# A fused attention and MLP kernel, rewritten with an order of engines from a model, wider exps, value bursts, paired key sums and token-major W2

## The chip, the cores and the metric

The kernel runs on one core of one Trainium2 chip. The metric is the device time of one execution in microseconds (us). Every time below is the median of several executions, with the lowest and highest of them. TensorE (PE) multiplies matrices, VectorE (DVE) and ScalarE (ACT) work on elements, GpSimd (POOL) does small work, and SyncE (SP) issues DMA transfers. Both kernels write the results of matmuls to PSUM, an on-chip tensor that they divide into eight banks.

## The reference, cut to what matters

```python
def _layernorm(x, eps=1e-5):
    m = mean(x); v = var(x)
    return (x - m) / sqrt(v + eps)

x  = A_x                                   # 2048 tokens x 1024, bf16
xn = _layernorm(x)
# A: attention, 32 heads of 32
q, k, v = split(xn @ wqkv)
s = softmax(q @ k.T * 32 ** -0.5) @ v @ wo
# B: MLP with a layer norm of its own, F = 3584
y = _layernorm(xn)                         # so x is normalised twice
g = silu(gelu(y @ w1 + b1) @ w2 + b2)
return x + s * g
```

The second norm of an already normalised token is only a scale s per token. With v the first variance and r = 1/sqrt(v + eps), the scale is 1/sqrt(v r r + eps). Both kernels use that, in different ways.

Attention is cut into 512 units. A unit is one group of four heads, 256 queries and 256 keys. It has 8 score matmuls, exps over 128 x 2048 values, and then value matmuls and matmuls with a matrix of ones, which sum the exps for the softmax's denominator. A query group is eight units with the same heads and queries.

## The kernel before

The order of instructions is written by hand: scores and exps of unit b, values of unit b-2, then dense matmuls (projections or MLP) up to a budget of time.

```python
for bl in range(NBH):                                # one unit
    ...                                              # 8 score matmuls into 4 of 5 PSUM banks
    for j in range(4):                               # four exps of 128 x 512
        add("scalar", lambda en, ...: en.activation(Pb[b % NPB][:, j, :], bank(bk), ACT.Exp, scale=SCALE), ...)
    if b >= 2:
        emit_pv(b - 2)                               # values and ones of one unit, in one accumulator bank
    ...                                              # dense matmuls for per_batch_ns
```

```python
# emit_pv, at the end of a query group: the reciprocal of 256 columns, then the product
add("vector", lambda en: en.reciprocal(rc_t[ri][:], ps[:, ACCB * 512 + 256:ACCB * 512 + 256 + QW]), ...)
add("vector", lambda en: en.tensor_tensor(OT[:, hg, ...], ps[:, ACCB * 512:ACCB * 512 + QW], rc_t[ri][:], op=ALU.mult), ...)
```

```python
# prologue: the normalised x and the doubly normalised x, each transposed on TensorE (256 transposes)
add("vector", lambda e, ...: e.tensor_scalar(xnb[i2][:], xt, lnp[:, tb, 2:3], lnp[:, tb, 3:4], op0=ALU.mult, op1=ALU.add), ...)
add("gpsimd", lambda e, ...: e.tensor_scalar(ybb[i2][:], xt, lnp[:, tb, 6:7], lnp[:, tb, 7:8], op0=ALU.mult, op1=ALU.add), ...)
```

The softmax here doesn't subtract the row's maximum and nothing guards it: scores larger than these inputs give would overflow.

Of the kernel before, what the change touches and what calls it, by code (L numbers as in the profile page):

```python
# [12 lines left out]
ENGS = ("sync", "gpsimd", "tensor", "vector", "scalar")  # L13


class _Sched:

    def __init__(self, nc, stack):
        self.nc = nc
        self.stack = stack  # L20
        self.ops = {e: [] for e in ENGS}
        self.sems = {}
        self.counts = {}

    def sem(self, name):
        if name not in self.sems:
            self.sems[name] = self.stack.enter_context(self.nc.semaphore(name))
            self.counts[name] = 0
        return name

    def cnt(self, name):
        return self.counts.get(name, 0)

    def add(self, eng, fn, waits=(), inc=None, dma=False):
        val = None
        ws = []
        if inc is not None:
            self.sem(inc)
            if dma and self.counts[inc] > 0:
                ws.append((inc, self.counts[inc]))  # L40
            self.counts[inc] += 16 if dma else 1
            val = self.counts[inc]
        for w in waits:
            if w is None:
                continue
            s, v = w
            if v is None or v <= 0:
                continue
            self.sem(s)
            ws.append((s, v))  # L50
        self.ops[eng].append((fn, tuple(ws), inc, dma))
        return val

    def emit(self, eng_name, eng):
        waited = {}
        for fn, waits, inc, dma in self.ops[eng_name]:
            for (s, v) in waits:
                if waited.get(s, 0) >= v:
                    continue
                eng.wait_ge(self.sems[s], v)  # L60
                waited[s] = v
            if fn is None:
                continue
            ins = fn(eng)
            if inc is not None:
                ins.then_inc(self.sems[inc], 16 if dma else 1)


def bass_recurrent_scan__mha_block__mixer_channel_mlp__prompt_kernel(
# [10 lines left out]
):  # L80
    _, S, D = A_x.shape
    F = B_w1.shape[1]
    DH = 32
    H = D // DH
    HG = H // 4
# [3 lines left out]
    QW = 256  # L89
    NQB = S // QW  # L90
    NKBP = S // 256
    CW = 256
    NCH = S // CW
    NH5 = D // 512
    EPS = 1e-5
    SCALE = DH ** -0.5
    W1P = 256
    NPC = F // W1P
    FBP = W1P // 128
    NPB = 4  # L100
    assert HG == DC and S % 512 == 0 and F % W1P == 0 and D % 512 == 0 and NT % 4 == 0

    x2 = A_x.rearrange("b s d -> (b s) d")
    out2 = out.rearrange("b s d -> (b s) d")

    with ExitStack() as st:
        sc = _Sched(nc, st)
        add = sc.add

        def sb(name, shape, dt):  # L110
            return st.enter_context(nc.sbuf_tensor(name, list(shape), dt))

        yT_d = nc.dram_tensor("yT_scratch", (128, DC, S), BF16).ap()
        g_d = nc.dram_tensor("g_scratch", (S, D), BF16).ap()

        ident = sb("ident", [128, 128], BF16)
        iota_i = sb("iota_i", [128, 128], I32)
        ones = sb("ones", [128, 32], BF16)
        xnT = sb("xnT", [128, DC, S], BF16)
        OT = sb("OT", [128, HG, S], BF16)  # L120
        QT = [sb(f"QT{i}", [128, S], BF16) for i in range(2)]
        KT = [sb(f"KT{i}", [128, S], BF16) for i in range(2)]
        Vh = [sb(f"Vh{i}", [128, NT, 128], BF16) for i in range(2)]
        wsl = [sb(f"wsl{i}", [128, DC, 3, 128], BF16) for i in range(2)]
        Pb = [sb(f"Pb{i}", [128, 4, 512], BF16) for i in range(NPB)]
        ar_state = {"off": 0}
        ARENA_ELEMS = (2 * DC * CW + 2 * DC * W1P + FB * CW + 2 * FB * 128 + DC * CW + 2 * D
                       + 3 * (6 * FBP * CW) + 3 * (4 * CW))
        arena = sb("arena", [128, ARENA_ELEMS], BF16)

        def carve(shape, dt, reset=False):
            if reset:
                ar_state["off"] = 0
            n = 1
            for d_ in shape[1:]:
                n *= d_
            nbf = n * (2 if dt == F32 else 1)
            off = ar_state["off"]
            ar_state["off"] += nbf
            assert ar_state["off"] <= ARENA_ELEMS, (ar_state["off"], ARENA_ELEMS)  # L140
            v = arena[:, off:off + nbf]
            if dt == F32:
                v = v.bitcast(F32)
            if len(shape) == 3:
                v = v.rearrange("p (a b) -> p a b", a=shape[1])
            return v

        yTc = [carve([128, DC, CW], BF16) for i in range(2)]
        w1p = [carve([128, DC, W1P], BF16) for i in range(2)]
        off_hT = ar_state["off"]  # L150
        hT = carve([128, FB, CW], BF16)
        off_after_hT = ar_state["off"]
        if FB * CW >= 4 * D + 2 * DC * 128:
            ar_state["off"] = off_hT
            xnb = [carve([128, D], BF16) for i in range(2)]
            ybb = [carve([128, D], BF16) for i in range(2)]
            yTs = [carve([128, DC, 128], BF16) for i in range(2)]
            assert ar_state["off"] <= off_after_hT
            ar_state["off"] = off_after_hT
        else:  # L160
            xnb = [sb(f"xnb{i}", [128, D], BF16) for i in range(2)]
            ybb = [sb(f"ybb{i}", [128, D], BF16) for i in range(2)]
            yTs = [sb(f"yTs{i}", [128, DC, 128], BF16) for i in range(2)]
        w2s = [carve([128, FB, 128], BF16) for i in range(2)]
        gT = carve([128, DC, CW], BF16)
        gst = [carve([128, D], BF16) for i in range(2)]
        xb_t = [carve([128, FBP * CW], F32) for i in range(3)]
        u_t = [carve([128, FBP * CW], F32) for i in range(3)]
        th_t = [carve([128, FBP * CW], F32) for i in range(3)]
        zh_t = [carve([128, CW], F32) for i in range(3)]  # L170
        th2_t = [carve([128, CW], F32) for i in range(3)]
        ofin = [carve([128, 512], F32, reset=(i == 0)) for i in range(2)]
        obf = [carve([128, D], BF16) for i in range(2)]
        NTB = 4
        xnT_flat = xnT[:].rearrange("p c s -> p (c s)")
        wo_sb = xnT_flat[:, 0:HG * D].rearrange("p (c n) -> p c n", c=HG)
        xres = [xnT_flat[:, HG * D + i * D: HG * D + (i + 1) * D] for i in range(NTB)]
        gres = [xnT_flat[:, HG * D + (NTB + i) * D: HG * D + (NTB + i + 1) * D] for i in range(NTB)]
        assert HG * D + 2 * NTB * D <= DC * S
        rc_t = [sb(f"rc{i}", [128, QW], F32) for i in range(2)]  # L180
        b1T = sb("b1T", [128, FB], F32)
        b2h = sb("b2h", [128, DC], F32)
        stats = sb("stats", [128, NT, NH5, 6], F32)
        mv = sb("mv", [128, NT, 2], F32)
        lnp = sb("lnp", [128, NT, 8], F32)
        ps = st.enter_context(nc.psum_tensor("ps", [128, 8 * 512], F32))
# [3 lines left out]

        def bankb(i):
            return ps[:, i * 512:(i + 1) * 512].bitcast(BF16)

        ACCB = 5
        NRING = 5

        add("gpsimd", lambda e: e.iota(iota_i[:], pattern=[[1, 128]], base=0, channel_multiplier=-1), inc="c_iota")
        add("vector", lambda e: e.tensor_single_scalar(ident[:], iota_i[:], 0, op=ALU.is_equal),
            waits=[("c_iota", 1)], inc="c_ident")
        add("vector", lambda e: e.memset(ones[:], 1.0), inc="c_ones")  # L200
        add("gpsimd", lambda e: e.dma_start(b1T[:], B_b1.rearrange("(fb p) -> p fb", p=128)), inc="c_b1", dma=True)
        add("gpsimd", lambda e: e.dma_start(b2h[:], B_b2.rearrange("(nb p) -> p nb", p=128)), inc="c_b2", dma=True)
        add("vector", lambda e: e.tensor_scalar_mul(b2h[:], b2h[:], 0.5), waits=[("c_b2", 16)], inc="c_b2h")

        def evy(tb):
            return ("ev_xyd", tb + 1)

        xst_v = OT[:].rearrange("p g s -> p (g s)")
        for tb in range(NT):
            add("sync" if tb % 2 == 0 else "gpsimd",  # L210
                lambda e, tb=tb: e.dma_start(xst_v[:, tb * D:(tb + 1) * D], x2[tb * 128:(tb + 1) * 128, :]),
                inc=f"x_ld{tb % 4}", dma=True)
        HALF = NT // 2 if NT >= 8 else NT

        def emit_stats(tb):
            xt = xst_v[:, tb * D:(tb + 1) * D]
            for c in range(NH5):
                add("vector", lambda e, tb=tb, c=c, xt=xt: e.bn_stats(stats[:, tb, c, :], xt[:, c * 512:(c + 1) * 512]),
# [578 lines left out]
```

## Time and profile before

The kernel before took 1485.49 us (1482.51 to 1490.63, three runs).

| | before |
|---|---|
| span of the profiled run | 1486.1 us |
| PE / ACT / DVE busy | 1205.9 / 1143.5 / 702.2 us |
| until the first exp | 107 us |
| 512 units | 107 to 1400 us, 2.53 us each |
| after the last unit | 86 us, ACT idle |

These lines are from the page of the kernel before: the busy time of the engines with its share of the span; the chain of work that ended last, by engine; and three of the costliest groups. A group reads: line, engine, operation, tiles and shapes, count, then busy us, mean ns of one, and the idle time just before it with what ended most of it.

```profile
PE 1205.9 (81%) x30330; PEld 801.9 (54%) x30336; DVE 702.2 (47%) x1173; ACT 1143.5 (77%) x2246; POOL 102.7 (7%) x119
...
PE 40%; ACT 18%; DVE 17%; DMA 14%; issue 10%; POOL 1%; DVEq 0%; SPq 0%; ACTq 0%; POOLq 0%
...
L695 ACT ACTIVATE Pb<-ps 128x512 bf16<-128x512 f32 x2048 | 1058.7, 609 | 173.2 <-PE ps L686 166.1
...
L302 PE MATMUL ps<-arena 128*32 128x256 bf16 x14336 | 494.0, 282 | 87.9 <-DMA arena<-in_B_w_dram 66.8
...
L612 DVE RECIPROCAL rc<-ps 128x256 f32<-128x256 f32 x64 | 112.4, 1756 | 145.8 <-PE ps L605 145.8
```

No engine is full, and the chain passes from one to another. ScalarE's 2048 exps wait for scores, TensorE's dense matmuls wait 66.8 us for weights, and each query group ends with a reciprocal of 1.76 us.

The view of the waits gives engine, line, what it waited for, us in total, times, and the longest.

```profile
PEld ps L686 <- ACT Pb L695: 186.4, 402, 2.9
...
PE ps L302 <- DMA arena<-in_B_w_dram: 66.8, 58, 5.3
```

**An accounting of TensorE's span.** It is worked out from the trace. Matmuls stream at 109 ns for a quad of four with 256 columns and 216 ns for a quad with 512 (start to start in the timeline; the few transposes are counted in proportion). A burst of scores uses another tiling of the array than everything else. In the trace of before, the time from the last column quad to the scores is about 320 ns in the median where the next quad would take 109, and from the scores to the values 0.11 us more than streaming, so I count 0.325 us a burst for the two switches. What remains of the span is called rest: TensorE waits, or runs at half clock. For the kernel before: streaming 970, switches 166, rest 350 us (71 until 107 us, 269 in the middle, 10 after 1422 us).

### The profile page before, as it was taken

To read this page: it belongs to the slowest core of one execution; us is meant where nothing else is said; L and a number is where in the kernel's file an instruction comes from. 1 tells how busy PE (TensorE), PEld (TensorE's weight loads), DVE (VectorE), ACT (ScalarE), POOL (GpSimd) and SP (SyncE) were. 2 spreads that over 40 slices of the span, in tenths; PEclk is the share of its full clock that TensorE was granted. 3 is DMA by queue.
4 is the path that set the end of the run, shared out by engine and by line. 5 is a ranking of instruction groups with operands and counts; after the bars stand their busy time and mean duration, and the time that the engine had idled before them with its cause. 6 is when DMAs were issued, how large, how long until landed. Compare 5 with 4: busy or idle time off the path is not lost.

```text
span 1486.1 us, 65842 instructions
## 1 busy us (share of the span) xinstructions
PE 1205.9 (81%) x30330; PEld 801.9 (54%) x30336; DVE 702.2 (47%) x1173; ACT 1143.5 (77%) x2246; POOL 102.7 (7%) x119
## 2 busy tenths in 40 slices
PE   2589878887889878987798878988798878777887
PEld 1455656555556545565555555655455655555643
DVE  6532862257422772347522683238522682277233
ACT  1229988897889888988898989988898987687600
POOL 3320000000000100001000100001000000000057
PEclk9999999999999989999899999999999998998999
DMA  6350457125560556045524562165307556535764
GB/s 135 71 129 3 119 119 143 41 60 141 111 144 3 137 123 120 9 101 149 105 52 86 137 158 52 31 145 148 83 5 143 135 163 124 120 116 123 145 198 163
DMA packets 388676, 159.44 MB, mean 107 GB/s; under 512 B 255280, under 2 KB 378160, under 8 KB 388400
## 3 DMA queue, kind: packets, MB, share of 16 engines
q1 hardware_dynamic: 378640, 138.43, 40.6%
q0 software_dynamic: 9760, 16.80, 4.3%
q8 instruction: 238, 3.90, 1.1%
q14 instruction: 38, 0.31, 0.1%
HBM read 142.62 MB, written 12.58 MB: 104 GB/s over the span
## 4 chain that ended last, share of the span: by engine, by line
PE 40%; ACT 18%; DVE 17%; DMA 14%; issue 10%; POOL 1%; DVEq 0%; SPq 0%; ACTq 0%; POOLq 0%
ACT Pb L695 18%; PE ps L302 17%; DMA arena<-in_B_w_dram 13%; PE ps L686 7%; DVE rc L612 6%; PE ps L599 6%; PE ps L605 4%; PE ps L732 3%; DVE arena L441 3%; DVE arena L446 2%; PE ps L269 2%; DVE OT L614 1%; PE ps L383 1%; DVE arena L448 1%; DVE arena L450 1%
## 5 line engine op out<-in xcount | busy, mean ns | idle before, releaser
L695 ACT ACTIVATE Pb<-ps 128x512 bf16<-128x512 f32 x2048 | 1058.7, 609 | 173.2 <-PE ps L686 166.1
L302 PE MATMUL ps<-arena 128*32 128x256 bf16 x14336 | 494.0, 282 | 87.9 <-DMA arena<-in_B_w_dram 66.8
L302 PEld LDWEIGHTS ps<-arena 128*32 128x32 bf16 x14336 | 394.2, 100 | 129.7 <-issue 82.7
L599 PE MATMUL ps<-Pb,Vh 128*32 128x256 bf16 x4096 | 273.8, 285 | 47.9 <-DVE OT L614 38.5
L605 PE MATMUL ps<-Pb,ones 128*32 128x256 bf16 x4096 | 270.1, 281 | 7.8 <-issue 7.7
L686 PE MATMUL ps<-QT,KT 32*128 32x256 bf16 x4096 | 211.5, 280 | 74.5 <-ACT Pb L695 59.0
L599 PEld LDWEIGHTS ps<-Pb,Vh 128*32 128x32 bf16 x4096 | 110.2, 96 | 169.8 <-issue 111.8
L612 DVE RECIPROCAL rc<-ps 128x256 f32<-128x256 f32 x64 | 112.4, 1756 | 145.8 <-PE ps L605 145.8
L686 PEld LDWEIGHTS ps<-QT,KT 32*128 32x128 bf16 x4096 | 61.9, 93 | 219.4 <-ACT Pb L695 186.4
L494 DVE TENSOR_SCALAR arena<-ps,b2h 128x256 f32<-128x256 f32 x64 | 30.9, 482 | 271.9 <-PE ps L302 271.9
L302 PE MATMUL ps<-xnT,wsl 128*32 128x512 bf16 x2048 | 130.8, 388 | 2.1 <-DMA wsl<-in_A_wqkv_dram 2.1
L441 DVE TENSOR_SCALAR arena<-ps,b1T 128x256 f32<-128x256 f32 x224 | 97.9, 479 | 72.7 <-PE ps L302 70.6
L605 PEld LDWEIGHTS ps<-Pb,ones 128*32 128x32 bf16 x4096 | 112.1, 98 | 9.0 <-issue 6.4
L527 POOL DMA_DIRECT2D g_scratch<-arena x16 | 8.9, 558 | 1291.5 <-DVE arena L525 1291.1
L456 ACT ACTIVATE arena<-arena 128x512 f32<-128x512 f32 x112 | 72.3, 646 | 23.9 <-DVE arena L450 23.9
L446 DVE TENSOR_TENSOR arena<-arena 128x512 f32<-128x512 f32 x112 | 77.6, 693 | 12.4 <-DVE arena L441 0.9
L450 DVE TENSOR_TENSOR arena<-arena 128x512 f32<-128x512 f32 x112 | 77.6, 692 | 3.9
L302 PEld LDWEIGHTS ps<-xnT,wsl 128*32 128x32 bf16 x2048 | 55.3, 99 | 41.9 <-issue 6.8
L461 DVE SCALAR_TENSOR_TENSOR arena<-arena 128x512 bf16<-128x512 f32 x112 | 75.1, 685 | 3.4 <-ACT arena L456 3.1
L269 PE MATMUL ps<-ident,arena 128*128 128x128 bf16 x256 | 30.5, 312 | 49.3 <-DVE arena L256 49.3
L383 PE MATMUL ps<-wsl,xnT 128*128 128x128 bf16 x1024 | 67.8, 220 | 0.0
L383 PEld LDWEIGHTS ps<-wsl,xnT 128*128 128x128 bf16 x1024 | 57.4, 98 | 14.2 <-issue 13.8
(47 smaller groups left out, 520.2 us busy)
## 6 DMA issues: line engine op xcount, KB each, us to landing
arena<-in_B_w_dram SPq DMA_DIRECT2D x112, 512.0 KB, 4.0
arena<-in_B_w_dram SPq DMA_DIRECT2D x64, 896.0 KB, 6.9
wsl<-in_A_wqkv_dram POOLq DMA_DIRECT2D x24, 256.0 KB, 6.8
yT_scratch<-arena SPq DMA_DIRECT2D x16, 256.0 KB, 2.8
arena<-yT_scratch SPq DMA_DIRECT2D x8, 512.0 KB, 8.6
g_scratch<-arena POOLq DMA_DIRECT2D x16, 256.0 KB, 2.6
xnT<-in_A_x_dram SPq DMA_DIRECT2D x16, 256.0 KB, 3.0
xnT<-g_scratch SPq DMA_DIRECT2D x16, 256.0 KB, 3.8
```

Source lines behind the costliest of these rows:

```text
L302: add("tensor", lambda e, j=j: e.matmul(out_fn(j), lhsT=lhsT_fn(j), rhs=rhs, start=start, stop=stop, tile_position=(0, 32 * j), skip_group ...
L383: mms.append((lambda w, inc, DB, dc=dc, tb=tb, t4=t4: add("tensor", lambda e: e.matmul(bank(DB, t4 * 128, (t4 + 1) * 128), lhsT=xnT[:, dc, ...
L441: add("vector", lambda e, k=k, fb=fb: e.tensor_scalar(xb_t[gi][:, k * CW:(k + 1) * CW], bank(DB, k * CW, (k + 1) * CW), b1T[:, fb:fb + 1], ...
L446: add("vector", lambda e: e.tensor_tensor(u_t[gi][:], xb_t[gi][:], xb_t[gi][:], op=ALU.mult), waits=va, inc="gl_b")
L450: add("vector", lambda e: e.tensor_tensor(u_t[gi][:], u_t[gi][:], xb_t[gi][:], op=ALU.mult), waits=[("gl_b", sc.cnt("gl_b"))], inc="gl_u")
L456: add("scalar", lambda e: e.activation(th_t[gi][:], u_t[gi][:], ACT.Tanh, scale=0.7978845608028654), waits=[("gl_u", vu)], inc="gl_t")
L461: add("vector", lambda e: e.scalar_tensor_tensor(hT[:, pi * FBP:(pi + 1) * FBP, :], th_t[gi][:].rearrange("p (k t) -> p k t", k=FBP), 1.0, ...
L599: add("tensor", lambda en, j=j, kb=kb, kbh=kbh, firstg=firstg: en.matmul(ps[32 * j:32 * j + 32, ACCB * 512:ACCB * 512 + QW], lhsT=Vh[i2][: ...
L605: add("tensor", lambda en, j=j, kbh=kbh: en.matmul(ps[32 * j:32 * j + 32, ACCB * 512 + 256:ACCB * 512 + 256 + QW], lhsT=ones[:, 0:32], rhs ...
L612: add("vector", lambda en: en.reciprocal(rc_t[ri][:], ps[:, ACCB * 512 + 256:ACCB * 512 + 256 + QW]), waits=[("pe_pv", b + 1), ("dve_acc", ...
L686: add("tensor", lambda en, j=j, kb=kb, kbh=kbh, bk=bk, qb=qb, i2=i2: en.matmul(bank(bk, kbh * 256, (kbh + 1) * 256), lhsT=KT[i2][32 * j:32 ...
L695: add("scalar", lambda en, j=j, bk=bk, b=b: en.activation(Pb[b % NPB][:, j, :], bank(bk), ACT.Exp, scale=SCALE), waits=[("pe_s", b + 1), ( ...
```

## The change

The intent is to keep TensorE busy all the time. The kernel is rewritten: its operations are declared with their data dependences, a model with durations simulates the engines, and the order that the model finds is recorded, engine by engine, and emitted. The order alone comes from the model; on the chip each instruction waits for its semaphores. Besides that:

- exps are 1024 wide (1024 instead of 2048), with six PSUM banks for scores and two for everything else;
- values and ones of a query group come in bursts, opened after the exps of its sixth unit;
- VectorE adds the exps of the two key blocks of a unit, so that the ones-matmuls halve;
- W2's product has tokens on the partitions, so that g needs no transpose;
- the second norm is no longer computed and transposed; its scale s is stored to memory, read back as a broadcast, and multiplied into the transposed xn (128 transposes fewer);
- W_o runs inside the last head group.

The diff is 1700 lines. Its core, with cuts marked by dots:

```diff
+        def commit(o, t):
+            if e == "SP":
+                tf[e] = t + o.occ
+                state["bw"] = max(state["bw"], t) + o.nbytes / 170.0     # the model's transfer rate, bytes per ns
+                o.fin = state["bw"] + 1900.0
...
+        def pe_step(t):
+            if o.mode != state["mode"]:
+                start += 100.0                                            # the model's price of a switch of tiling, ns
...
+        def unit(u, pv):
+            for h in range(2):
+                x = act(lambda e, h=h: e.activation(P[pi][:, 2 * h:2 * h + 2]..., ps[:, pr[h] * 1024:(pr[h] + 1) * 1024], ACT.Exp, scale=SCALE), ...)
+            pa = dve(lambda e: e.tensor_tensor(PA[ai][:], P[pi][:, :, 0, :], P[pi][:, :, 1, :], op=ALU.add), ...)
...
+                pv.trigger = xs[5] if g < HG * NQB - 1 else xs[0]         # when a value burst may open
...
-            add("gpsimd", lambda e, ...: e.tensor_scalar(ybb[i2][:], xt, lnp[:, tb, 6:7], lnp[:, tb, 7:8],
-                                                         op0=ALU.mult, op1=ALU.add), ...)
+                pool(lambda e, t=t: e.tensor_scalar(xnb[t % 4], xst[t], mv[:, t, 0:1], lnp[:, t, 1:2],
+                                                    op0=ALU.subtract, op1=ALU.mult), 950, ...)
...
+        dma("s_st", lambda e: e.dma_start(s_d.rearrange("(t p) -> p t", p=128), lnp[:, :, 3]), 8192, [("s3",)], [("s_d",)])
+        dma("b1", lambda e: e.dma_start(b1T[:], B_b1.rearrange("(fb p) -> p fb", p=128)), 8192, [("s3",)], [("b1",)])
+        dma("b2", lambda e: e.dma_start(b2b[:], B_b2...to_broadcast([128, D])), 262144, [("s3",)], [("b2",)])
...
+            dma("sbc", lambda e: e.dma_start(sbc[:], s_d[c * 256:(c + 1) * 256]...to_broadcast([128, 256])), 131072, [("s_d",)], [("sbc",)])
```

All DMA is now issued from SyncE's single queue, in the recorded order.

## The prediction

> **What bounds the kernel now.** No engine is saturated: the page gives PE 1205.9 us (81%), ACT 1143.5 us (77%), DVE 702.2 us (47%) of 1486.1 us. The chain of waits alternates: PE 40%, ACT 18%, DVE 17%, DMA 14%, issue 10%. By stretches: until 107 us no exp runs; 512 attention units take 107 to 1400 us, 2.53 us each; then 86 us of tail with ACT idle. Inside a unit (timeline): four 128x512 exps, 477 ns start to start, 2.06 us with drain; scores reuse five PSUM banks and wait for the previous exps (186 us in the waits). Per query group the value matmuls wait for a 1.76 us reciprocal and a multiply on the only accumulator bank (38 + 55 us); dense matmuls wait 67 us for double-buffered weights. TensorE runs at half clock in about 28 windows, mean granted clock 0.96.
>
> **What the change does to each engine** (counts from the instruction order, durations from the trace).
> - ACT: 2048 exps of 477 ns become 1024 of about 902 ns (estimate: 427 ns more for 512 more elements): 977 to 924 us. With 144 tanhs and 16 copies: about 1007 us.
> - PE: the ones-matmuls halve (-512 quads of 109 ns, -56 us); the y and g transposes go. Streaming: 5632 quads of 256 at 109 ns, 704 of 512 at 216 ns, scores 112 us, transposes 10 us: about 900 us. Some 497 score bursts stay. A burst switches row/column tiling twice: from last column quad to scores 318 instead of 109 ns, from scores to values 0.11 us above streaming, so 0.32 us, 160 us in all. The Trainium skill, "TensorEngine Tiling (Array Packing)", Key Properties, says that changing the tiling mode drains the array; the trace agrees. The model in the code books only 0.1 us per switch, so I expect PE about 60 us later than its plan. PE total about 1060 us: narrowly the new bound.
> - DVE: +512 pair sums (128x1024 bf16). None is in the trace; from the Trainium skill, "VectorE: DVE Perf Modes", perf-mode tier table (tensor_tensor in bf16 runs 2x), I estimate 0.6 to 0.7 us, +310 to 350 us. The big reciprocals (112 us) shrink to 8 columns. About 800 us, 70%: not bound.
> - DMA: about the same bytes; W2 rows double to 512 B, three and four buffers: the 67 us of waits mostly go.
>
> **On the critical path.** Prologue: exps run inside it, the first at about 20 us instead of 107; I charge 30 us of lost PE time. Tail: W_o runs inside the last head group, leaving 46 quads (10 us), norm and store: 15 us more. Middle: about 2.05 us per unit, since PE (2.0) and ACT (1.9) are nearly equal and in a fixed order each loses something to the other: 30 us. Sum: 1060 + 30 + 15 + 30 = 1135 us.
>
> **Prediction: 1135 us, range 1095 to 1190. Faster by over 2%: 0.97; within 2%: 0.02; slower: 0.01.**
>
> **What would show it.** First exp before 25 us; exp start-to-start near 902 ns; unit 2.0 to 2.15 us; PE idle small, switches its largest "issue" gaps; half-clock windows mostly gone; pair sum 0.6 to 0.7 us; ACT 85 to 92% busy.
>
> **What would make it wrong.** Pair sums at one element per cycle (1.1 us) would make DVE the bound, toward 1250. A DMA waiting in the single in-order queue and holding up weights, or a recorded order whose timing misses a little everywhere, gives 1200. If switches hide behind waits and the clock stays full, 1090.

## More of the kernel before

The next line is from the groups by form (every shape by itself). It is GpSimd's op of the prologue, which will matter later: it has the form multiply, then add, and one takes 1.2 us.

```profile
L259 POOL TENSOR_SCALAR arena<-OT,lnp 128x1024 bf16<-128x1024 bf16 x16 | 19.6, 1227 | 35.1 <-PE ps L269 23.3 <-DVE lnp L239 11.8
```

## The result and the profile after

The changed kernel took **1228.68 us** (1225.87 to 1232.59, four runs), the kernel before on the same chip 1486.53 us. The ratio is 0.8262, with a 95% interval of 0.8229 to 0.8294. Ratios are the mean time of one kernel's runs over that of the other's of the same rounds, so not quite the ratio of the medians quoted. All outputs are right. The prediction of 1135 us was right that the kernel gets much faster, and too low by 94 us; the result lies outside its range.

From the page of the changed kernel: busy time, granted TensorE clock in 40 slices (tenths), the chain, and two groups.

```profile
PE 1069.9 (87%) x30080; PEld 717.9 (59%) x30080; DVE 848.6 (69%) x1531; ACT 1040.2 (85%) x1186; POOL 71.2 (6%) x34
...
PEclk8876999999999999999999999999999998789999
...
PE 49%; ACT 37%; POOL 5%; DVE 5%; issue 3%; SPq 1%; DMA 1%; POOLq 0%; ACTq 0%; DVEq 0%
...
L871 ACT ACTIVATE P<-ps 128x1024 bf16<-128x1024 f32 x1024 | 976.5, 1111 | 136.6 <-PE ps L862 135.9
L874 DVE TENSOR_TENSOR PA<-P 128x1024 bf16<-128x1024 bf16 x512 | 351.7, 688 | 210.1 <-ACT P L871 204.3
```

The engines' work is as predicted: exps follow each other in 903 ns (902 predicted), and a pair sum takes 688 ns (0.6 to 0.7 us predicted). The clock row has two dents, at the start (slices 1 to 4) and at slices 34 to 36.

The accounting of TensorE says where 89 of the 94 us are; it adds up to the span of the profiled run, 1224.1 us, and not to the median of the runs (us):

| | predicted | measured |
|---|---|---|
| streaming | 900 | 899.7 |
| switches of tiling (994, charged) | 160 | 161.5 |
| rest, 0 to 115 us (prologue) | 30 | **74.0** |
| rest, 115 to 1010 us (middle) | 30 | 39.7 |
| rest, 1010 to 1110 us (late dip) | none | **39.3** |
| rest, from 1110 us (tail) | 15 | 9.9 |
| sum | 1135 | 1224.1 (span) |

So two stretches hold nearly all of it.

**What the row of the switches hides.** Its 161.5 us are only a count times the price that the prediction used, so that it had to agree. One burst of the changed kernel (timeline of PE from 400 us; start, length, instruction):

```profile
403.16 0.61 PE L544 MATMUL ps<-yT,w1r 128*32 128x256 bf16 x16
403.71 0.40 PE L862 MATMUL ps<-qk 32*128 32x256 bf16 x8
404.03 0.40 PE L544 MATMUL ps<-yT,w1r 128*32 128x256 bf16 x8
```

The first line's four quads stream for 436 ns, until 403.60, and the scores start 0.11 us later. Two score quads stream for 218 ns, and the next column quad starts 0.10 us after them. This is typical: of 394 entries into scores after a quad of 256 columns, 309 have no exp that ended in the 60 ns before, and there the median from quad to scores is 216 ns. In the kernel before, 233 of 364 such entries start within 60 ns after the end of an exp; they waited for it, and the 318 ns contain this wait. So two switches cost about 0.21 us a burst, 104 us for 497 bursts. The other 57 us of the row are waits, nearly 50 of them in the middle, whose rest is then about 88 us. Only the sum of the two rows was foreseen, 190 us predicted for switches and middle and 201 measured.

**The clock.** The two stretches are also the two dents of the clock. The records of the clock show half clock for 82 us in the changed kernel, in seven pieces. Before each piece lie 3.4 us in which TensorE was busy for 0 to 44% of the time (worked out from the matmuls' times).

The table of stretches shows the same (start:end, length, busy us and instructions of PE, PEld, DVE, ACT, POOL, then granted clock, DMA share, GB/s):

```profile
0.00:115.00 115.00, 58.21 (x1236) 41.79 (x1236) 41.62 (x86) 32.41 (x34) 71.18 (x34) 0.78 0.34 88
115.00:900.00 785.00, 734.89 (x21656) 507.08 (x21656) 593.86 (x1061) 742.37 (x854) 0.00 (x0) 1.00 0.47 133
...
1010.00:1110.00 100.00, 71.82 (x1856) 45.79 (x1844) 56.16 (x100) 77.08 (x87) 0.00 (x0) 0.85 0.49 150
```

PE is 94% busy in the middle (734.89 of 785), 51% in the prologue and 72% in the late dip.

**The prologue.** All of GpSimd's 71.18 us lie there. Its op of the layer norm, by form:

```profile
L667 POOL TENSOR_SCALAR gw<-hT,mv,lnp 128x1024 bf16<-128x1024 bf16 x10 | 37.7, 3781 | 0.5
...
L667 POOL TENSOR_SCALAR gw<-w2r,mv,lnp 128x1024 bf16<-128x1024 bf16 x6 | 23.0, 3836 | 0.3 <-PE ps L644 0.2
```

The op has the size of the 1.23 us op of before, on the same engine, and takes 3.8 us. Sixteen of them are 61 us of work with 0.8 us of idle time before them, and every token tile has to pass this chain. The waits show what comes after it:

```profile
ACT P L871 <- PE ps L862: 135.9, 81, 26.4
...
PE ps L862 <- DVE qk L634: 25.2, 3, 23.6
DVE yT L718 <- DMA sbc<-s_scratch: 24.6, 1, 24.6
...
PEld ps L544 <- DVE xb L738: 16.1, 29, 1.6
```

VectorE stands 24.6 us for one transfer, TensorE 23.6 us for VectorE, and ScalarE 26.4 us for TensorE. The timeline from 70 us to 100 us shows that it is one event (start us, length us, engine, line, op; in brackets the idle time before it and its releaser):

```profile
74.44 0.37 SPq L684 DMA_DIRECT2D s_scratch<-lnp  x1
74.86 0.94 SPq L685 DMA_DIRECT2D b1T<-in_B_b_dram  x1
75.84 11.06 SPq L686 DMA_DIRECT2D b2b<-in_B_b_dram  x1
86.94 1.04 SPq L711 DMA_DIRECT2D w2r<-in_B_w_dram  x2
88.02 9.81 SPq L715 DMA_DIRECT2D sbc<-s_scratch  x2
94.37 1.90 DVE L718 TENSOR_TENSOR yT<-big,sbc 128x512 bf16<-128x512 bf16 x3 [24.57 <-DMA sbc<-s_scratch]
96.18 0.68 DVE L634 CAST qk<-ps 128x512 bf16<-128x512 f32 x1
...
96.92 0.61 PE L862 MATMUL ps<-qk 32*128 32x256 bf16 x8 [23.62 <-DVE qk L634]
```

The scale is stored at 74.4 us and its broadcast is issued at 88.0 us. VectorE's recorded order has the multiplication by it ahead of a copy that the next scores need, so all three engines stand.

**The late dip.** From the timeline of PE at 1034 us:

```profile
1034.61 0.61 PE L862 MATMUL ps<-qk 32*128 32x256 bf16 x8 [1.13 <-ACT P L871]
1036.44 0.61 PE L862 MATMUL ps<-qk 32*128 32x256 bf16 x8 [1.22 <-ACT P L871]
1038.28 0.61 PE L862 MATMUL ps<-qk 32*128 32x256 bf16 x8 [1.22 <-ACT P L871]
```

Here the recorded order has score bursts alone, so that TensorE waits for the exps. Elsewhere dense matmuls stand between them. At the start of the last head group, six reloads of the attention output (512 KB each) are issued from 1019 us on, and W_o (2 MB) at 1047 us. The model believes that 170 bytes move per ns, so it thinks that weights queued behind these loads come late, and it records no dense work there (argued here, and tested below). The chip moved about 350 bytes per ns between 1020 and 1030 us.

### The profile page after: what moved, and what is told of

It is laid out like the page before. It is cut to its first block, busy times and chain, and to the rows that moved or that the text cites. A ratio compares the mean times of both kernels' runs of the same rounds, so it can differ in the third digit from the quotient of the medians.

```text
span 1224.1 us, 63652 instructions
## 1 busy us (share of the span) xinstructions
PE 1069.9 (87%) x30080; PEld 717.9 (59%) x30080; DVE 848.6 (69%) x1531; ACT 1040.2 (85%) x1186; POOL 71.2 (6%) x34
## 4 chain that ended last, share of the span: by engine, by line
PE 49%; ACT 37%; POOL 5%; DVE 5%; issue 3%; SPq 1%; DMA 1%; POOLq 0%; ACTq 0%; DVEq 0%
PE ps L544 41%; ACT P L871 34%; PE ps L862 8%; POOL gw L667 4%; ACT ut L746 2%; SPq L686 1%; DVE PA L874 1%; ACT gw L779 1%; DVE nt L901 1%; DMA sbc<-s_scratch 1%; DVE xb L738 0%; POOL lnp L664 0%; PE ps L644 0%; DVE V L617 0%; DVE ut L744 0%
## 5 line engine op out<-in xcount | busy, mean ns | idle before, releaser
L871 ACT ACTIVATE P<-ps 128x1024 bf16<-128x1024 f32 x1024 | 976.5, 1111 | 136.6 <-PE ps L862 135.9
L874 DVE TENSOR_TENSOR PA<-P 128x1024 bf16<-128x1024 bf16 x512 | 351.7, 688 | 210.1 <-ACT P L871 204.3
L544 PE MATMUL ps<-yT,w1r 128*32 128x256 bf16 x7168 | 238.6, 273 | 12.7 <-DVE QKT L831 3.9
L544 PE MATMUL ps<-w2r,hT 128*32 128x256 bf16 x7168 | 232.3, 273 | 12.0 <-issue 5.2
L544 PEld LDWEIGHTS ps<-yT,w1r 128*32 128x32 bf16 x7168 | 178.5, 96 | 55.4 <-issue 29.5
L544 PEld LDWEIGHTS ps<-w2r,hT 128*32 128x32 bf16 x7168 | 182.4, 97 | 41.7 <-issue 27.4
L544 PE MATMUL ps<-P,V 128*32 128x256 bf16 x4096 | 170.7, 280 | 16.8 <-issue 8.6
L544 PE MATMUL ps<-big,qk 128*32 128x512 bf16 (+1 forms) x2304 | 141.5, 374 | 14.5 <-ACT big L647 8.5
L544 PE MATMUL ps<-qk,big 128*32 128x256 bf16 (+1 forms) x3072 | 137.1, 318 | 6.7 <-DVE gw L775 1.4
L862 PE MATMUL ps<-qk 32*128 32x256 bf16 x2048 | 104.7, 277 | 40.6 <-DVE qk L634 25.2
L544 PEld LDWEIGHTS ps<-P,V 128*32 128x32 bf16 x4096 | 104.9, 98 | 45.1 <-ACT P L871 18.1
L544 PE MATMUL ps<-PA,ones 128*32 128x256 bf16 x2048 | 126.4, 277 | 1.9 <-issue 1.6
L544 PEld LDWEIGHTS ps<-qk,big 128*32 128x32 bf16 x3072 | 77.8, 99 | 46.3 <-issue 13.1
L544 PEld LDWEIGHTS ps<-big,qk 128*32 128x32 bf16 x2304 | 57.5, 102 | 63.3 <-issue 15.1
L738 DVE TENSOR_TENSOR xb<-ps,b1T 128x512 bf16<-128x512 f32 x112 | 76.8, 686 | 14.2 <-PE ps L544 13.7
L544 PEld LDWEIGHTS ps<-PA,ones 128*32 128x32 bf16 x2048 | 57.3, 98 | 22.7 <-issue 13.7
```

The costliest lines, as they stand in the source:

```text
L544: ins = e.matmul(dst(j), lhsT=lhsT(j), rhs=rhs(j), start=start, stop=stop, tile_position=(0, 32 * j), skip_group_check=True)
L738: dve(lambda e: e.tensor_tensor(xb_t[i3][:].rearrange("p (k t) -> p k t", k=2), bank(it.bank).rearrange("p (k t) -> p k t", k=2), b1T[:, 2 ...
L862: ins = e.matmul(bank(b0[j], kk * 256, (kk + 1) * 256), lhsT=QKT[sl][32 * j:32 * j + 32, 1, kb * 128:(kb + 1) * 128], rhs=QKT[sl][32 * j:3 ...
L871: x = act(lambda e, h=h: e.activation(P[pi][:, 2 * h:2 * h + 2].rearrange("p j k q -> p (j k q)"), ps[:, pr[h] * 1024:(pr[h] + 1) * 1024], ...
L874: pa = dve(lambda e: e.tensor_tensor(PA[ai][:], P[pi][:, :, 0, :], P[pi][:, :, 1, :], op=ALU.add), c_b16(1024), [("P", pi, 0), ("P", pi, 1 ...
```

## The experiments

Each was run beside the kernel before on the same chip. "Rest" is that of the accounting above.

### The form of GpSimd's op

```diff
-  e.tensor_scalar(xnb[t % 4], xst[t], mv[:, t, 0:1], lnp[:, t, 1:2], op0=ALU.subtract, op1=ALU.mult)   # (x - m) r
+  e.tensor_scalar(xnb[t % 4], xst[t], lnp[:, t, 1:2], lnp[:, t, 5:6], op0=ALU.mult, op1=ALU.add)       # x r + (-m r)
```

> The changed kernel with one edit: the layer norm on POOL computes x*r + (-m*r) (mult, add, as the kernel before) instead of (x-m)*r (subtract, mult). Theory A (the form of the op makes it slow): the 16 ops fall from 3.78 to about 1.2 us, the first 115 us shorten by 25 to 40 us, time 1190 to 1203 us. Rival B (something else of the place, such as its source tiles or VectorE at the same time): the op stays near 3.8 us and the time at 1228. Rival C (the prologue is held by the 8 KB store and reload of the second-norm scale, not by POOL): the op is fast, but the stall at 73 to 97 us only moves forward and the time falls by under 15 us.

Measured: 1202.11 us (1197.91 to 1205.12), ratio 0.8118 (0.8085 to 0.8151), so 27 us less by the medians and 21 us by the ratios. From its groups by form:

```profile
L671 POOL TENSOR_SCALAR gw<-hT,lnp 128x1024 bf16<-128x1024 bf16 x10 | 11.9, 1195 | 0.5
L671 POOL TENSOR_SCALAR gw<-w2r,lnp 128x1024 bf16<-128x1024 bf16 x6 | 7.6, 1266 | 1.6 <-PE ps L644 1.5
```

The op takes a third of the time, and the prologue's rest falls from 74 to 47 us. By the medians this is the larger of the two gains from one edit (the other is 22 us, further below), but their intervals overlap.

### The scale stored per token pair, biases at the start

```diff
-  s3 for all 16 tiles after the last pair; s_st (2048 x 4 bytes), then b1, b2
+  b1, b2 before everything; for each pair of tiles: s3, s_st (256 x 4 bytes)
```

> The changed kernel with one edit: the second-norm scale is computed and stored per pair of token tiles, and the two bias loads go out at the start, so that the first MLP chunk waits for no store behind small packets; POOL's slow op stays. Theory C (that DMA chain costs the 24 us stall of TensorE at 73 to 97 us): 1203 to 1213 us. Theory A alone (POOL's 16 slow ops hold the prologue): the last tiles are normalised no earlier, so TensorE waits for them instead and the time falls by under 12 us.

Measured: 1223.54 us (1220.39 to 1224.79), ratio 0.8261. That is 5 us by the medians, and nothing by the ratio. With the slow GpSimd op still there, it is no lever.

### Both together

> Both edits, fast POOL form and per-pair scale. If the two losses are separate and both real, 1228 minus 45 to 60 us: 1168 to 1185 us, the first 32 units done by about 115 us instead of 166. If they are two views of one loss, about the better of the two runs.

Measured: 1206.19 us (1198.75 to 1210.13), ratio 0.8141 (0.8103 to 0.818), not better than the first alone. The early scale did not arrive early: in the recorded order its broadcast stood behind other issues until 60 us. TensorE also had two standstills. One, of 5.4 us, ended with a copy of VectorE that had itself waited 4.9 us for nothing that the profile shows ("remote"); the other, of 3.2 us, lay in the middle of a dense group ("issue"). They fell into the time of the small-packet transfers. Their cause stays open.

### The model's transfer rate

```diff
-                state["bw"] = max(state["bw"], t) + o.nbytes / 170.0
+                state["bw"] = max(state["bw"], t) + o.nbytes / 300.0
```

This changes no instruction, only the recorded order.

> The changed kernel with one number of its model altered: DMA 300 instead of 170 bytes per ns, so that the recorded order no longer leaves TensorE with score bursts alone while it believes the weights to be queued behind the 5.6 MB of reloads of the last head group. The DMAs themselves stay. Theory D (the dip at 1020 to 1110 us is written into the order): it goes, 1228 minus 20 to 35 us, 1193 to 1208. Rival E (the weights are really late there, the queue being full): TensorE waits for the weight DMAs instead and the time stays within 10 us of 1228.

Measured: 1206.66 us (1200.21 to 1211.9), ratio 0.8136 (0.8098 to 0.8174), so 22 us less by the medians and 19 us by the ratios. The stretch from 1010 to 1110 us of this kernel, to be held against the one of the changed kernel shown above:

```profile
1010.00:1110.00 100.00, 87.64 (x2604) 62.37 (x2600) 63.73 (x114) 87.38 (x101) 0.00 (x0) 0.97 0.65 196
```

Now 2604 matmuls fit into it instead of 1856, and the rest there falls from 39.3 to 14.2 us. So the late dip was a hole in the recorded order, made by the model's rate; the rival, weights that are really late, would have kept it. Part of the gain is given back: the middle's rest is 53.8 instead of 39.7 us.

### Both fixes

> The changed kernel with both repairs that worked alone: the mult-add form on POOL (-26 us alone) and DMA at 300 bytes per ns in the model (-22 us alone). Losses at two ends of the run, so they should add: 1176 to 1186 us. If the order recorded for the start does not fit any more, above 1195.

Measured: 1195.13 us (1192.31 to 1195.68), ratio 0.8057 (0.801 to 0.8103). The gains, 27 and 22 us, add to 34, not 49 (by the ratios 21 and 19 add to 30, not 40). Prologue 52 us and dip 14 us are about those of the single fixes. What is missing is the middle: 52 us instead of 39.7. A new order is new everywhere.

### And the switches charged at 0.32 us a burst

```diff
-                start += 100.0
+                start += 212.0 if state["mode"] == "c" else 112.0
```

> The same, with the model charging 212 ns for a switch from column to row tiling and 112 ns back instead of 100 and 100[...]. Theory F (the mispriced switch costs time because the recorded order runs late against the engines): the unaccounted TensorE time of the middle, 8 us in 200, falls and the total goes 10 to 25 us below e5. Rival G (in the middle TensorE is simply full: streaming plus switching is 96% of the time, and an order cannot remove that): within 8 us of e5.

Measured: 1188.55 us (1186.11 to 1189.03), ratio 0.8008 (0.7968 to 0.8047). The new order is worth some 7 us: both versions ran on the same chip, and their runs do not overlap. That lies within the 8 us of the rival and below the 10 to 25 us of the theory. The number of switches hardly moved (1018 to 1020). Nor is the new charge truer, since 212 ns into the scores contains the wait described above, and without it the trace shows 107 ns. Why this order is better stays open.

### Exps of 512 again

The edit, in words:

```diff
-  one activation of 128 x 1024 per half unit
+  two activations of 128 x 512 per half unit
```

> One part of the change undone: each 1024-wide exp is issued as two of 512 (2 x 477 instead of 903 ns). ScalarE gets 52 us more work. If TensorE is the bound of the middle: 1228 plus 0 to 20 us. If ScalarE is (it is 95% busy there): plus 35 to 55 us.

Measured: 1227.81 us (1225.67 to 1230.0), ratio 0.8276 (changed kernel: 0.8262). The wide exps move the time by nothing, although ScalarE's busy time grows from 1040 to 1100 us. By stretches the rest of the middle grew by 13 us and that of the dip shrank by 10 us, so the zero could be a sum of two effects. The run was therefore repeated on the version with both fixes:

> The 1024-wide exps undone again, now on the two-fix version (1195 us, ratio 0.8057), where neither the slow GpSimd op nor the late stretch of score bursts alone is left. In the changed kernel the undo cost 0 us, as the sum of about 13 us lost in the stretch from 115 us to 900 us and 10 us won back in the stretch from 1010 us to 1110 us. Theory (the wide exps are worth something, hidden by another order in that late stretch): 1203 to 1212 us, ratio 0.811 to 0.818. Rival (ScalarE has room everywhere): within 5 us of 1195, ratio 0.802 to 0.809.

Measured: 1200.12 us (1199.71 to 1201.3), ratio 0.8087 (0.8033 to 0.814), against 0.8057 (0.801 to 0.8103); the intervals overlap. The middle's rest is 52.6 against 52.1 us, so the 13 us did not come back, and my theory falls. The rest from 1010 to 1110 us is 20.6 against 14.1 us, so what this trace lost lies there. What can be said is that the wide exps are worth some 5 us here by the medians, which the ratios do not tell from nothing. ScalarE, 85% busy in the changed kernel and 90% in the undo on it, has room.

### Without the pair sums

The edit, in words:

```diff
-  pa = dve(... PA = P[:, :, 0, :] + P[:, :, 1, :]); one quad with ones
+  two quads with ones
```

> One part undone: no pair sums on VectorE, two ones-matmul groups per unit instead of one. TensorE gets 512 x 109 ns = 56 us more, VectorE 350 us less. If TensorE is the bound of the middle: 1228 plus 40 to 58 us. If it has slack: under plus 20; if VectorE's pair sums were in the way, below 1228.

Measured: 1264.96 us (1257.69 to 1269.5), ratio 0.8522 (0.847 to 0.8573), so 36 us more. Streaming grew by 56 us, from 899.7 to 955.6, and the rest fell by 23 us, from 162.9 to 139.7. So TensorE is the bound, but not wholly: the kernel lost about 0.65 us for each added microsecond of TensorE work. Two things are mixed in this: added work can fill waits, and VectorE, with 849 us of work before the edit and 548 after it, can cause fewer waits. The run does not part them.

### Value bursts opened early

```diff
-  pv.trigger = xs[5] if g < HG * NQB - 1 else xs[0]
+  pv.trigger = xs[1] if g < HG * NQB - 1 else xs[0]
```

> Undoes the value bursts per query group: the value and ones matmuls of a query group may open as soon as the exp of its second unit is placed (as the changed kernel, otherwise), instead of its sixth. Theory (the burst matters, through the banks): six of the eight PSUM banks belong to scores, so a value accumulator that stays open for eight units instead of three leaves one bank for the dense matmuls, and each dense item then waits for the copy of the one before; the switches of tiling stay near 1000. Expect 1290 to 1350 us, with TensorE's time outside streaming and switches in the stretch from 115 us to 900 us more than 80 us, against 34 us in the changed kernel. Rival (the burst saves only switches, and there were as many before): within 15 us of 1228.

Measured: 1308.29 us (1304.51 to 1312.3), ratio 0.8813 (0.8757 to 0.8869), so 80 us more. The rest from 115 to 900 us is 93 us instead of 34. The number of switches is 1018, near the 994 of the changed kernel. One of the waits that grew, to be held against the same line of the changed kernel above (16.1 us, 29 times):

```profile
PEld ps L544 <- DVE xb L738: 37.6, 68, 1.2
```

So the burst is worth much, and not through switches. The theory is that while a value accumulator is open, one bank is left for dense work, and each dense item waits for the copy of the one before. From 115 to 900 us TensorE's own waits for these copies (five lines of the view) grew from 16 to 41 us, which agrees. But its waits at L544 for exps grew too, from 3 to 15 us: value matmuls now open before their exps are there. With 5 us more of waits before scores, this is most of what the view names of the 59 us. So the banks are the larger part that is seen, and not shown to be the whole.

### Four forms of GpSimd's op in one kernel

The edit, in words:

```diff
+  t % 4 == 0: subtract, mult   (operands in two tiles, as in the change)
+  t % 4 == 1: subtract, mult   (operands in one tile)
+  t % 4 == 2: mult, subtract   (operands in one tile)
+  t % 4 == 3: mult, add        (operands in one tile)
```

> One look at the form of the layer norm's op on GpSimd, four forms in one kernel, by token tile modulo 4, otherwise as the two-fix version: 0: subtract then mult with the two per-partition operands in two tiles (the change's form); 1: subtract then mult with both operands in one tile; 2: mult then subtract, both in one tile; 3: mult then add, both in one tile (1.20 us in the first experiment). Theory A (a subtract as first operation is slow): 0 and 1 take 3.8 us, 2 and 3 take 1.2 us. Rival B (any subtract is slow): 0, 1 and 2 take 3.8 us. Rival C (two tiles of operands are slow): only 0 takes 3.8 us. Results stay correct in all forms.

1203.16 us, a single run. From its groups by form, where L674, L678, L682 and L686 are the forms 0, 1, 2 and 3:

```profile
L678 POOL TENSOR_SCALAR gw<-hT,lnp 128x1024 bf16<-128x1024 bf16 x3 | 12.2, 4069 | 0.0
L674 POOL TENSOR_SCALAR gw<-hT,mv,lnp 128x1024 bf16<-128x1024 bf16 x3 | 11.4, 3793 | 0.0
...
L682 POOL TENSOR_SCALAR gw<-hT,lnp 128x1024 bf16<-128x1024 bf16 x2 | 7.6, 3788 | 0.2
...
L686 POOL TENSOR_SCALAR gw<-hT,lnp 128x1024 bf16<-128x1024 bf16 x2 | 2.4, 1194 | 0.0
```

Rival B holds: each of the three forms with a subtract takes 3.8 to 4.1 us, first or second, and where the operands lie does not matter. Of these four only mult, add takes 1.2 us; a form with add and no mult was not tried.

### The second cause of the prologue, in four steps

With the op mended, 52 us of rest remained in the prologue, and VectorE still waited 17.5 us for the broadcast of the scale. The first attempt stored the scale per pair again, now with the biases after the fourth pair.

> The version with three changes (1188.5 us, ratio 0.8008) with, besides, the scale of the second norm computed and stored per token pair, and the two bias loads sent after the fourth pair: it removes the 17.5 us wait for the broadcast scale before the first MLP item. In the trace of that version TensorE's rest in the first 115 us is 52 us. Theory (that wait costs TensorE time): rest below 42 us and 1174 to 1182 us, ratio 0.791 to 0.797. Rival (as in the run with the pair-wise scale and the early bias loads: TensorE then stands for nothing visible elsewhere, and the gain is lost): 1185 to 1195 us, with standstills of 2 us and more in the middle of dense groups before 70 us.

Measured: 1189.19 us (1187.48 to 1193.08), ratio 0.8014, no gain; the prologue's rest was 56.2 us. In its trace the broadcast was issued at 39.3 us, right behind the b2 load, whose issue had lasted 10.4 us, and it landed 11.5 us later. So the suspicion fell on the bias loads. They were moved alone:

```diff
-  dma("b1", ..., [("s3",)], ...);   dma("b2", ..., [("s3",)], ...)
+  dma("b1", ..., [("rs", 2)], ...); dma("b2", ..., [("rs", 2)], ...)
```

> The changed kernel with one difference: the loads of the two biases are sent as soon as the third token pair's scale is known (about 20 us), when SyncE's queue has nothing else to do, instead of after the second norm's scale (74 us), where the load of 3584 two-byte values holds up the issue behind it for 11 us and the scale's broadcast comes after both. Theory (that queue is the second cause of the long prologue): VectorE's wait for the broadcast falls from 24.6 us to 6 to 10 us, TensorE's rest in the first 115 us falls from 74 us by 10 to 16 us, and the kernel takes 1211 to 1220 us. Rival (TensorE has nothing else to do there, as the last run suggests): the wait falls, but the time stays within 4 us of 1228.7.

> The version with three changes (GpSimd op as mult then add, transfer rate 300 and switches charged in the model; 1188.5 us, ratio 0.8008) with the bias loads sent early as well. There the wait for the broadcast is 17.5 us. Theory: the wait falls to 4 to 8 us, TensorE's rest in the first 115 us from 52 us to 40 to 46 us, and the kernel takes 1177 to 1184 us, ratio 0.793 to 0.798, the fastest of this study. Rival: within 3 us of 1188.5, ratio 0.799 to 0.803.

Measured: in the changed kernel 1224.58 us (1219.98 to 1226.06), ratio 0.8259; in the version with three changes 1180.47 us (1176.81 to 1185.22), ratio 0.7978 (0.7948 to 0.8007). So by the medians the move gives 4 us and 8 us. By the ratios it gives nothing in the changed kernel (0.8259 against 0.8262) and 0.003 in the other version, whose intervals overlap and whose two runs were on two chips. The waits only fell from 24.6 to 19.5 us and from 17.5 to 14.0 us, and are twice as long as expected. The reason is in the view of the DMA issues (destination and source, count, KB each, us from issue to landing), first of the changed kernel, then of the kernel with the biases early:

```profile
s_scratch<-lnp SPq DMA_DIRECT2D x1, 8.0 KB, 12.2
b1T<-in_B_b_dram SPq DMA_DIRECT2D x1, 7.0 KB, 14.0
```

```profile
b1T<-in_B_b_dram SPq DMA_DIRECT2D x1, 7.0 KB, 4.5
s_scratch<-lnp SPq DMA_DIRECT2D x1, 8.0 KB, 10.9
```

Early, before that store, the load of 3584 two-byte values lands in 4.5 us (its packets take 2 us; in the version with four changes it took 8.3 us). The store of 2048 four-byte values takes 10.9 us even without the bias loads behind it, although its last packet is recorded 2.2 us after the issue. So the bias loads were slowest behind that store, and moving them leaves the larger part of the wait: my theory of the bias loads falls. With 256-packet stores per pair:

> The version with four changes (1180.5 us, ratio 0.7978) with the scale of the second norm computed and stored per token pair, so that the broadcast for the first 256 tokens depends on a store of 256 packets at about 20 us instead of one of 2048 packets at 40 us. Theory (the store's 11 us is what is left of VectorE's 14 us wait): that wait falls below 4 us, TensorE's rest in the first 115 us from 44 us to 34 to 41 us, 1170 to 1178 us, ratio 0.789 to 0.796. Rival (small packets beside dense work bring standstills elsewhere, as in the run with both GpSimd changes): 1179 us or more, with standstills of over 2 us in the middle of dense groups before 70 us.

Measured: 1181.2 us (1173.13 to 1183.56), ratio 0.7962 (0.7901 to 0.8023), no gain; the wait was 10.3 us. The one small store whose landing is recorded took 14.2 us, with the bias loads beside it, and in the first attempt the eight took 10.6 us in the median, so cutting the store into eight does not help. The last attempt left the number of bytes and changed the packets. One transpose on TensorE turns the 128 x 16 scales into 16 x 128, so that the store is 16 packets of 512 bytes:

```diff
-  dma("s_st", lambda e: e.dma_start(s_d.rearrange("(t p) -> p t", p=128), lnp[:, :, 3]), 8192, [("s3",)], [("s_d",)])
+  identf = ...; sT = ...                          # an identity in f32, and 16 x 128 for the result
+  sit = _Item("pro")
+  chunk(sit, lambda e, b: e.transpose(bank(b)[0:16, 0:128], lnp[:, :, 3], identf[:]), 300, [("s3",), ("identf",)], mode="t")
+  dve(lambda e: e.tensor_copy(sT[:], bank(sit.bank)[0:16, 0:128]), 250, [], [("sT",)], 0, sit)
+  pro_q.insert(15, sit)
+  dma("s_st", lambda e: e.dma_start(s_d.rearrange("(t p) -> t p", p=128), sT[:]), 8192, [("sT",)], [("s_d",)])
```

> The version with four changes once more, as the reference of the run after it on the same chip: 1180 us, ratio 0.795 to 0.801.

> The version with four changes (1180.5 us) with the scale of the second norm transposed on TensorE to 16 rows of 128 before it is stored, so that the store is 16 packets of 512 bytes instead of 2048 of 4 bytes; one transpose and one copy more. Theory (the four-byte store is the second cause): the store lands within 5 us of its issue instead of 11, VectorE's wait for the broadcast falls from 14 us to 5 to 9 us, and the kernel gains 3 to 7 us on the version with four changes. Rival (a store to memory that a load reads back is slow whatever its packets): the store still takes about 11 us, and the time stays within 2 us of the version with four changes.

Measured side by side: 1181.13 us (1176.38 to 1182.36), ratio 0.797 (0.7937 to 0.8004), and **1169.25 us** (1166.12 to 1170.46), ratio 0.7896 (0.7867 to 0.7925). From the timelines, the store, the broadcast and the first multiplication; first without, then with the 512-byte packets:

```profile
42.28 0.37 SPq L688 DMA_DIRECT2D s_scratch<-lnp  x1
...
52.81 0.34 SPq L719 DMA_DIRECT2D sbc<-s_scratch  x1
...
56.32 0.69 DVE L722 TENSOR_TENSOR yT<-big,sbc 128x512 bf16<-128x512 bf16 x1 [13.62 <-DMA sbc<-s_scratch]
```

```profile
42.97 0.35 SPq L695 DMA_DIRECT2D s_scratch<-sT  x1
...
44.39 0.35 SPq L726 DMA_DIRECT2D sbc<-s_scratch  x1
...
47.80 1.29 DVE L729 TENSOR_TENSOR yT<-big,sbc 128x512 bf16<-128x512 bf16 x2 [0.96 <-DMA sbc<-s_scratch]
```

From store to broadcast it is now 1.4 us instead of 10.5, VectorE's wait is 1.0 us instead of 13.6, and the prologue's rest is 37.5 us instead of 48.9. That is 11.4 of the 12 us gained. (Against the other trace of the version with four changes, with 43.9 us, it is 6.4 us of 7.7, so the share is firmer than the size.) The rival, that a store which a load reads back is slow whatever its packets, falls: the same 8 KB landed 1.4 us after issue. The gain is larger than the 3 to 7 us that I expected, because the wait vanished instead of halving. This is the fastest kernel.

### All runs

Times are medians; the rest is TensorE's, in us, by the stretches of the accounting.

| run | us | ratio | rest: prologue | middle | 1010 to 1110 | tail |
|---|---|---|---|---|---|---|
| the change | 1228.68 | 0.8262 | 74.0 | 39.7 | 39.3 | 9.9 |
| mult, add on GpSimd | 1202.11 | 0.8118 | 47.3 | 46.6 | 33.5 | 7.2 |
| scale per pair | 1223.54 | 0.8261 | 70.2 | 40.4 | 37.1 | 9.7 |
| both | 1206.19 | 0.8141 | 54.6 | 43.7 | 40.1 | 8.7 |
| transfer rate 300 | 1206.66 | 0.8136 | 69.9 | 53.8 | 14.2 | 7.1 |
| mult, add and rate 300 ("two fixes") | 1195.13 | 0.8057 | 52.0 | 52.1 | 14.1 | 7.0 |
| and switches charged ("three changes") | 1188.55 | 0.8008 | 51.7 | 50.2 | 10.6 | 8.1 |
| and biases early ("four changes") | 1180.47 | 0.7978 | 43.9 | 48.8 | 8.5 | 8.0 |
| four changes, once more | 1181.13 | 0.797 | 48.9 | 45.8 | 11.0 | 8.3 |
| four changes and 512-byte store | 1169.25 | 0.7896 | 37.5 | 46.8 | 9.1 | 8.1 |
| three changes, scale per pair | 1189.19 | 0.8014 | 56.2 | 51.5 | 10.0 | 8.2 |
| four changes, scale per pair | 1181.2 | 0.7962 | 47.9 | 46.7 | 9.6 | 8.1 |
| biases early, on the change | 1224.58 | 0.8259 | 70.2 | 39.1 | 38.0 | 9.6 |
| four forms, on two fixes (one look) | 1203.16 | none | 65.8 | 49.2 | 13.7 | 7.1 |
| exps of 512, on the change | 1227.81 | 0.8276 | 70.8 | 52.8 | 28.9 | 8.2 |
| no pair sums, on the change | 1264.96 | 0.8522 | 68.6 | 25.2 | 33.4 | 12.5 |
| early values, on the change | 1308.29 | 0.8813 | 78.4 | 107.3 | 12.9 | 46.8 |

The stretches are fixed in time, so a slower kernel has its late dip further on: that of the early values lies in the last column.

## Why the prediction was right or wrong

**Right: the work.** Streaming 899.7 us against 900 predicted (partly luck: the terms listed add up to 888, and the trace has 5760 quads of 256 columns where the prediction counts 5632), exps 903 ns against 902, pair sums 688 ns against 0.6 to 0.7 us, VectorE 69% busy against 70%, ScalarE 85%, the first exp at 21.7 us (before 25 us predicted). The Trainium skill's "TensorEngine Tiling (Array Packing)", Key Properties, says that a change of tiling mode drains the array, and this trace agrees: where no exp is waited for, 0.11 us more into the scores and 0.10 us more out of them. Its "VectorE: DVE Perf Modes", perf-mode tier table, gave the 2x of bf16 tensor_tensor on which the estimate of the pair sums rests; 688 ns for 1024 elements a partition agrees.

**Right: the bound.** TensorE is the bound, narrowly. Giving 56 us of work back to it cost 36 us (while VectorE was relieved, as said above), and taking the wide exps from ScalarE cost 0 to 5 us. Units in the middle took 2.12 us (from unit 32 at 166.0 us to unit 448 at 1048.8 us; 2.0 to 2.15 predicted).

**Wrong: "Prologue: exps run inside it ...; I charge 30 us of lost PE time".** It measured 74 us. The exps did run inside it, but two things were not costed. The first is GpSimd's op, which the change turned from mult, add into subtract, mult. The model's own line says 950 ns for it, the trace of before had 1227 ns for the old form, and the new form takes 3.8 us: 27 us of the prologue's rest, shown by the first experiment and narrowed to the subtract by the one with four forms. The second is the store of the scale. I booked "the y and g transposes go" as a saving and did not ask what replaces them; it is a round trip through memory with four-byte packets, 10.9 to 12.2 us until the store lands. It was worth 12 us in the version with four changes; in the changed kernel itself, with the slow op still there, the scale stored per pair brought nothing by the ratio.

**Wrong: the late dip, for which the sum has no term.** It measured 39.3 us. The prediction doubted the model's 0.1 us per switch, which was about right, and did not look at the model's transfer rate beside it. With 300 instead of 170 bytes per ns the dip is 14.2 us. The prologue and the dip together hold 83 us of what the sum missed.

**Wrong, but it cancelled: "A burst switches row/column tiling twice ... 0.32 us, 160 us in all".** The 318 ns were read where TensorE also waited for an exp. The switches cost about 104 us, and the model's 0.1 us for each was about right. The middle lost about 88 us in waits, where "each loses something to the other: 30 us" was charged. The two errors make up for each other by luck; the total hides both.

**Half right: "A DMA waiting in the single in-order queue ... gives 1200".** The risk was named, but for weights. What waited was the broadcast of the scale, and the store ahead of it held up the queue. The 67 us of waits for weights did go: the view of the waits after has no such line.

**Wrong: "half-clock windows mostly gone".** The changed kernel ran at half clock for 82 us, nearly all in the two stretches above (before: 116 us, in 23 pieces and not the 28 windows that the prediction counts). TensorE was at work in 46 of the 82 us, so that they cost it some 23 us (an estimate: half of the time at work). In the last version 10 us at half clock are left. The skill's "TensorE: Matmul & The Clock Gate", Part 1, says that the clock halves after an idle window of about 3.4 us; the records here show half clock in multiples of 3.4 us, but TensorE need not be idle for so long. Before the three pieces of the late dip it was busy for 39, 25 and 25% of the 3.4 us, with no gap over 1.9 us. Here the measurement decides: many short waits were enough.

**What stays open.** In the last version 37.5 us of rest in the prologue and 46.8 us in the middle (about 95 with the waits that the row of the switches hides) are not taken apart. The standstills in the middle of dense groups have no cause in the records. That the two fixes do not add is located in the middle of the new order, not explained.

## What to carry to other kernels

When an order is recorded from a model, every constant of the model is a claim about the chip: compare each (rates, prices of switches, durations by form) with the trace, since a wrong one leaves a hole in the order that no engine can close later. Read such a price only where nothing else is waited for: the 318 ns were a switch and a wait in one. When a change takes work away, cost what replaces it, and look at each op whose form changed, even where size and engine stay. Small packets belong on the list of suspects by their landing time, not by their bytes: read the time from a store's issue to the issue of what depends on it.

## What the Trainium skill lacked or had wrong

- "GPSIMD Engine Reference", section 3, Performance versus the Vector engine, gives cycles per element for the best loop and for two inputs, and says nothing of the form of a two-step op with scalars. Here, on 128 x 1024 bf16, mult, add takes 1.2 us, and each of the three forms with a subtract that were tried 3.8 to 4.1 us.
- "DMA: Bandwidth & Descriptors", Specifications, says that transfers below 512 B are not at line rate, and that a read-modify-write is done. It gives no time for a store of many tiny packets, which decides here: 2048 packets of 4 bytes landed 10.9 to 12.2 us after issue, the same 8 KB as 16 packets of 512 bytes after 1.4 us. A load of 3584 packets of 2 bytes landed in 4.5 to 8.3 us before that store and in 14.0 us behind it. (Where so many packets come from the same page does say, in Rules for kernel authors: a non-contiguous last dimension lowers to one descriptor per element. The traces agree: 3584 packets of 2 bytes for the 7 KB of b1.)
- "TensorEngine Tiling (Array Packing)", Key Properties, names the drain at a change of mode without a duration. Here it is 0.11 us from column to row tiling and 0.10 us back, where no exp is waited for.
